# Sparse attention with a feed-forward layer on one core: the spacing of the feed-forward steps and the planner's price of a matrix product

## The chip, the cores and the metric

The kernel runs on one core of one Trainium2 chip. The metric is the device time of one execution in microseconds (us). A core has TensorE (in the profile PE, and PEld for its weight loads), VectorE (DVE), ScalarE (ACT), GpSimd (POOL) and SyncE (SP), which issues the DMA transfers here. Each engine runs its own list of instructions in order and waits for the others by semaphores.

## The reference

```python
def _attn_ref(q, k, v, tau):                       # batch 8, heads 8, 576 rows, 64 columns
    scale = 1.0 / np.sqrt(q.shape[-1])
    scores = scale * np.matmul(q, k.transpose(0, 1, 3, 2))
    thresh = np.max(scores, axis=-1, keepdims=True) - tau
    scores = np.where(scores >= thresh, scores, -1000000000.0)
    scores = scores - np.max(scores, axis=-1, keepdims=True)
    attn = np.exp(scores)
    attn = attn / (np.sum(attn, axis=-1, keepdims=True) + 1e-09)
    return np.matmul(attn, v).astype(np.float32)

def _moe_ref(x, w_in, w_out, s, b):                # x 4608 x 512, w_in 512 x 2048, w_out 2048 x 512
    h = x @ w_in
    r = np.maximum(h, 0.0)
    g = s * (r * r) + b
    return (g @ w_out).astype(np.float32)
```

Attention keeps only scores within tau of each row's maximum. Its output, with the heads side by side, is x: 8 batches of 576 rows, 4608 rows of 512 columns, and goes through the feed-forward layer.

## The kernel before, in words

**Attention** is worked in 288 tiles of 128 query rows of one head (`tile_of`). On PE a tile has scores against 576 keys (L328), later five transposes of the weighted scores (L357 into the bank `tp`, L358 into `tt`), and a product with the values for each group of two tiles (L404 into the bank `pv`; some groups carry 64 more rows, the tail). In the first 36 tiles, batch 0, a plain float32 form is used (L373 in the place of L404). Between them stand, for each tile, the copy with the row minimum on DVE (L331), the exponential on ACT (L337), the mask with the row sum on DVE (L340), the normalisation on POOL (L348), and the split of the transposed tile into two float32r parts, high on ACT (L388, L390) and low on DVE (L391, L393), which empties `tp` and `tt` for the next tile. The products' result is copied (ACT L409) and completed (DVE L411) into the columns of x. Each head's keys, queries and values are loaded by SP and split in the same manner (ACT L278, L286, L291; POOL L279, L292; DVE L287).

**Feed-forward** is worked in 18 blocks of 256 rows of x (`Block`). 16 of them are "full" blocks, two for each batch, which come ready every 18 tiles on average (after tiles 15, 35, 53, 71, 89, 107, 125, 143 and so on, counted from 0); two more hold the tails of four batches each and come ready after tiles 143 and 287. A block is staged (`stage`): x is split into `xh` (ACT L518) and `xl` (DVE L520), two pieces each; there are two pairs of these buffers, so one block can be staged while the one before is in use. Then come 16 steps (`step`), one for each 128 of the 2048 inner columns. A step is twelve matmuls of 256 columns into the bank `h` (L535), then ACT's Relu, which empties the bank (L538), its square (L540), the high part `gh` (L541), the low part `gl` on POOL (L542; on DVE in the last block), and six matmuls of 512 columns into `o` (L548), three for each half of the rows. There is one bank for `h`; `g`, `gh` and `gl` have two buffers. After 16 steps the block is finished: DVE adds the bias (L559) and SP stores it. The weights stay in SBUF; each is loaded and split (L465 to L476) before its first step.

**The order of the work** is not written by hand. Every operation is put in a plan (`Plan.add`) with its engine, a cost as a pair (how long the engine is held, how long until the result can be used; in ns), what it reads and writes, and a number `at`, in tiles. `Plan.run` goes through the program with these costs: whenever an engine is free, it takes among the operations whose inputs are there the one with the smallest `at`. So `at` is a rank among ready work and not a time, and an engine never waits in the plan while something is ready. What comes out is a fixed list for each engine; on the chip, each engine follows its list and waits where an input isn't there.

For the blocks, `when` (L711) is the number that the first step of a block gets: at least 1.5 tiles after the tile that completes the block, and not before the steps of the block ahead are through. Step f of the block gets `when + each * f` (L719), so `each` is how many tiles lie between two steps; a block of 16 steps takes 16 x `each` tiles, while the blocks come 18 tiles apart. The staging gets `max(i + 1.5, when - 1)`. Attention's operations have the tile's own number, with small offsets. PE's cost is reckoned in `pe` (L183) from the number of matmuls and their columns.

Of the kernel before, what the change touches and what calls it, by code (L numbers as in the profile page):

```python
# [106 lines left out]
def tile_attention_ffn(ctx: ExitStack, tc: tile.TileContext, qT, kT, v, tau, w_in, w_out, s, b, out):  # L107
# [50 lines left out]
    plan = Plan()  # L158
# [21 lines left out]

    def pe(n, cols, fn, r, w, at):

        plan.add("PE", (n * (0.452 * cols + 1.5), n * (0.452 * cols + 1.5) + 170), fn, r, w, at)  # L183

    def dve(cost, fn, r, w, at, port=False):
        plan.add("DVE", cost, fn, r, w, at, port)
# [128 lines left out]
    def tile_of(ti, i):  # L315
# [7 lines left out]
        def scores():  # L323
            for hf in range(2):
                cs = slice(hf * HS, (hf + 1) * HS)
                seq = ti.st()
                for n, (stat, kk) in enumerate(seq):
                    nc.tensor.matmul(ps[:, hf, 0:HS], stat, kk[:, cs], start=(n == 0), stop=(n == len(seq) - 1))  # L328
        pe(2 if plain else 4 * len(ti.heads), HS * (3.7 if plain else 1), scores, ti.kq(), [bk], i - SCORES_AHEAD)

        dve((760, 840), lambda: nc.vector.tensor_scalar(  # L331
# [22 lines left out]
        def transposes():  # L354
            em = get()[1]
            for t in range(NQ):
                nc.tensor.transpose(out=tp[:, t, :], in_=em[:, t * P:(t + 1) * P], identity=ident)  # L357
            nc.tensor.transpose(out=tt, in_=em[:, M:S], identity=ident)  # L358
        pe(4.3, 240, transposes, [em_k, "ident"], ["tp", "tt"], i + 0.5)
        if plain:  # L360
            ke = ("e32", i % 2)

            def both():
                nc.scalar.copy(out=e32(i)[:, 0:NQ], in_=tp)
                nc.scalar.copy(out=e32(i)[0:T, NQ], in_=tt)
            act((660, 760), both, ["tp", "tt"], [ke], i + 0.5)
            for pr, j, cs, dest, key in plain:
                n = cs.stop - cs.start

                def products(pr=pr, j=j, cs=cs, n=n):  # L370
                    for kt in range(5):
                        ks = slice(0, P if kt < NQ else T)
                        nc.tensor.matmul(bank["pv"][0:D, 0:n], pr.get()[2][ks, j, kt], e32(i)[ks, kt, cs], start=(kt == 0),  # L373
                                         stop=(kt == 4))
                pe(5, n * 4, products, [ke, pr.keys[2 + j], pr.keys[2 + j] + (1,)], ["pv"], i + VALUES_AFTER)
                act((80 + 0.75 * n, 180 + 0.75 * n), lambda dest=dest, j=j, n=n: nc.scalar.copy(
                    out=dest[j * D:(j + 1) * D], in_=bank["pv"][0:D, 0:n]), ["pv"], [key], i + VALUES_AFTER)
            return
# [17 lines left out]
    def with_v(g, at):  # L396
        ps = bank["pv"][:, 0:g.n]
        j = g.hd.j
        ke = g.keys(0, g.n, ("eh", "el", "et"))
        def products():  # L400
            hi, lo = (lazy[x][:, :, g.c0:g.c0 + g.n] for x in ("ehi", "elo"))
            seq = [(kt, o) for kt in range(4) for o in (hi, lo)] + [(4, hi)]
            for n, (kt, o) in enumerate(seq):
                nc.tensor.matmul(ps, g.hd.v()[:, kt, :, :], o[:, kt], start=(n == 0), stop=(n == len(seq) - 1))  # L404
        pe(9, g.n, products, ke + g.hd.kvs, ["pv"], at)
        a, o = slice(j * D, (j + 1) * D), slice((1 - j) * D, (2 - j) * D)
        for off, n, dest, key in g.dests:
            kx = [key + (j, u) for u in range(2)] if key[0] == "x" else [key + (j,)]
            act((50 + 0.85 * n, 150 + 0.85 * n), lambda off=off, n=n, dest=dest: nc.scalar.copy(  # L409
                out=dest[a], in_=ps[o, off:off + n]), ["pv"], kx, at)  # L410
            dve((80 + 1.05 * n, 160 + 1.05 * n), lambda off=off, n=n, dest=dest: nc.vector.tensor_tensor(  # L411
                out=dest[a], in0=ps[a, off:off + n], in1=dest[a], op=ALU.add), ["pv"] + kx, kx, at)
# [68 lines left out]
    def sums(k, at):  # L481

        fs = range(4 * k, 4 * k + 4)

        def products():
            for n, (f, h) in enumerate((f, h) for f in fs for h in range(2)):
                nc.tensor.matmul(bank["h"], ones, wo[h][f], start=(n == 0), stop=(n == 7))  # L487
        pe(8, DM, products, [(f"w{f}", "o") for f in fs] + ["ones"], ["h"], at)
        if k == 0:
            act((520, 620), lambda: nc.scalar.copy(out=bias_t, in_=bank["h"]), ["h"], ["bias"], at)  # L490
        else:
            dve((620, 700), lambda: nc.vector.tensor_tensor(out=bias_t, in0=bank["h"], in1=bias_t, op=ALU.add),
                ["h", "bias"], ["bias"], at)
        if k == 3:
            act((560, 660), lambda: nc.scalar.mul(out=bias_t, in_=bias_t, mul=b_t), ["bias", "b"], ["bias"], at)
# [76 lines left out]
    def make_block(kind, a, hf):  # L572
        if kind == "full":
            r = a * S + hf * NB
            k = xs[a, hf]
            return Block(xb[k], [("x", k, c, j, i) for c in range(NP) for j in range(2) for i in range(2)],
                         [[(0, P, out[r + t * P:r + (t + 1) * P, :])] for t in range(2)], (a, hf) == (B - 1, 1))
        return Block(xt, [("xt", bi, c, j) for bi in range(4) for c in range(NP) for j in range(2)],
                     [[(j * T, (j + 1) * T, out[(4 * a + 2 * t + j) * S + M:(4 * a + 2 * t + j + 1) * S, :])
                       for j in range(2)] for t in range(2)], False)  # L580
# [75 lines left out]
    tiles, first = [], {}  # L656
# [37 lines left out]
    def convert(f):  # L694
        if f not in converted:
            converted.add(f)
            load_weights(f, 2 + f)
            weights(f, WEIGHTS_AT + WEIGHTS_EACH * f)
# [4 lines left out]
    for i, ti in enumerate(tiles):  # L703
        ti.tag = "o" if i < TWO_BANKS and i % 2 else "s"

        events.append((i, lambda ti=ti, i=i: tile_of(ti, i)))
        for g in () if ti.plain else ti.end:
            events.append((i + 0.1, lambda g=g, i=i: with_v(g, i + VALUES_AFTER)))
        if True:
            for k_ in ti.blocks:  # L710
                when = max(when, i + FFN_AFTER)  # L711
                each = 1.125 if i < len(tiles) // 2 else 1.0

                def block(k_=k_, when=when, step=step, i=i, each=each):
                    blk = make_block(*k_)
                    blk.stage(max(i + FFN_AFTER, when - 1))
                    for f in range(NF):
                        convert(f)
                        blk.step(f, when + each * f)  # L719
                        if not step and f % 4 == 3:  # L720
                            sums(f // 4, when + each * f)
                    blk.finish(when + each * (NF + 1))

                events.append((max(i, n_plain) + 0.2, block))
                when += each * NF
                step += NF
# [47 lines left out]
```

## Time and profile before

| What | us |
|---|---|
| Three runs | 1429.4, 1423.86, 1428.97; median 1428.97 |
| Profiled execution | 1427.36 |
| Its span, first to last instruction | 1425.4 |
| PE busy | 1392.9 (98%), 9328 matmuls |
| Weight loads busy | 1255.2 (88%) |
| DVE busy | 1074.0 (75%) |
| ACT busy | 991.4 (70%) |
| POOL busy | 730.5 (51%) |
| Mean granted clock of TensorE | 0.994 |

Durations come from the profiled execution. A busy PE is not a PE at its peak: matmuls are pipelined, so that one is listed with 0.28 us or more while the next begins 0.12 us after it; how fast PE goes is read from start to start. Idle time listed before an instruction is measured from those modelled ends. The numbers in the names of buffers (`xh_3604`) are set anew for each program and only tell buffers apart within one.

### The profile page before, as it was taken

How to read it: one execution, taken by the hardware profiler on the slowest of the kernel's cores; microseconds unless marked ns; L12 is line 12 of the kernel's file. 1: busy time of each engine (PE TensorE's matmuls, PEld its weight loads, DVE VectorE, ACT ScalarE, POOL GpSimd, SP SyncE). 2: the span in 40 equal slices, each digit the busy share in tenths (PEclk: the TensorE clock that was granted, in tenths of full speed). 3: DMA queues.
4: the chain of work that ended last, by engine and by line, in shares of the span. 5: the costliest groups of instructions: out<-in, count | busy, mean ns of one | idle time of the engine just before them, and what ended most of it. 6: DMA issues, size and time to landing. Idle time of an engine off the chain costs nothing.

```text
span 1425.4 us, 29320 instructions
## 1 busy us (share of the span) xinstructions
PE 1392.9 (98%) x9328; PEld 1255.2 (88%) x9328; DVE 1074.0 (75%) x3099; ACT 991.4 (70%) x2487; POOL 730.5 (51%) x798
## 2 busy tenths in 40 slices
PE   8999999999999999999999999999999999999998
PEld 5677789898898989898999999999999999999887
DVE  4877777988888887988789887888788787886101
ACT  3777667777777767777677777776777777776443
POOL 1223345656565556656566556665556556653210
PEclk9999999999999999999999999999999999999999
DMA  8610011322222221322222222222222222220000
GB/s 294 246 39 21 23 58 52 95 58 61 60 79 73 59 79 52 95 59 62 64 66 80 70 72 65 80 65 63 63 75 69 76 57 70 61 85 1 16 16 15
DMA packets 94539, 99.58 MB, mean 70 GB/s; under 512 B 34480, under 2 KB 72368, under 8 KB 94384
## 3 DMA queue, kind: packets, MB, share of 16 engines
q1 hardware_dynamic: 94384, 97.71, 23.1%
q8 instruction: 73, 1.20, 0.3%
q14 instruction: 82, 0.67, 0.1%
HBM read 88.21 MB, written 9.44 MB: 69 GB/s over the span
## 4 chain that ended last, share of the span: by engine, by line
PE 92%; DVE 5%; issue 1%; ACT 1%; POOL 0%; DMA 0%; DVEq 0%; SPq 0%; ACTq 0%; POOLq 0%
PE h L535 28%; PE o L548 27%; PE s L328 12%; PE tp L357 9%; PE pv L404 9%; PE pv L373 4%; PE tt L358 2%; DVE em L340 1%; DVE e L391 1%; PE o L328 1%; PE h L487 1%; DVE xl L520 1%; DVE oo L559 0%; DVE e L393 0%; DVE x L411 0%
## 5 line engine op out<-in xcount | busy, mean ns | idle before, releaser
L535 PE MATMUL h<-xh,w 128*128 128x256 f32 x2304 | 471.1, 287 | 2.8 <-ACT xh L518 1.7
L535 PEld LDWEIGHTS h<-xh,w 128*128 128x128 f32 x2304 | 380.9, 192 | 13.0 <-ACT g L538 3.3
L348 POOL TENSOR_SCALAR em<-em,st 128x576 f32<-128x576 f32 x288 | 251.8, 874 | 272.6 <-DVE st L345 116.5
L548 PE MATMUL o<-w,gh 128*128 128x512 f32 x1152 | 370.0, 402 | 0.9 <-ACT g L538 0.5
L542 POOL TENSOR_TENSOR gl<-g,gh 128x256 fp32r<-128x256 f32 x272 | 213.2, 784 | 276.6 <-ACT gh L541 117.7
L535 PE MATMUL h<-xl,w 128*128 128x256 f32 x1152 | 328.8, 285 | 7.3 <-DVE xl L520 7.3
L340 DVE SCALAR_TENSOR_TENSOR em<-sm,st,em 128x577 f32<-128x577 f32 x288 | 253.0, 878 | 42.1 <-ACT em L337 32.0
L331 DVE TENSOR_SCALAR_CACHE_REDUCE sm<-s 128x576 f32<-128x576 f32 x280 | 211.2, 754 | 94.3 <-PE s L328 91.8
L337 ACT ACTIVATE em<-sm,st 128x576 f32<-128x576 f32 x288 | 224.9, 781 | 33.6 <-DVE sm L331 32.6
L538 ACT ACTIVATE g<-h 128x256 f32<-128x256 f32 x288 | 109.3, 380 | 194.9 <-PE h L535 189.1
L535 PEld LDWEIGHTS h<-xl,w 128*128 128x128 f32 x1152 | 221.8, 193 | 13.4 <-DVE xl L520 8.7
L548 PE MATMUL o<-w,gl 128*128 128x512 f32 x576 | 226.3, 393 | 0.0
L548 PEld LDWEIGHTS o<-w,gh 128*128 128x128 f32 x1152 | 195.7, 189 | 25.6 <-issue 1.2
L391 DVE TENSOR_TENSOR e<-tp,e 128x512 fp32r<-128x512 f32 (+1 forms) x280 | 178.2, 636 | 50.0 <-ACT e L388 44.9
L279 POOL TENSOR_TENSOR k<-rk,k 128x576 fp32r<-128x576 f32 x112 | 169.8, 1516 | 52.8 <-ACT k L278 48.4
L388 ACT CAST e<-tp 128x512 fp32r<-128x512 f32 (+1 forms) x280 | 151.0, 539 | 63.8 <-PE tp L357 60.2
L357 PE MATMUL tp<-ident,em 128*128 128x128 f32 x1152 | 176.8, 276 | 7.7 <-DVE e L391 4.7
L328 PE MATMUL s<-k,q 128*128 128x288 f32 x896 | 166.3, 308 | 0.8 <-DVE sm L331 0.8
L357 PEld LDWEIGHTS tp<-ident,em 128*128 128x128 f32 x1152 | 138.2, 141 | 32.4 <-POOL em L348 6.2
L404 PE MATMUL pv<-e,v 128*128 128x320 f32 (+1 forms) x1008 | 154.1, 296 | 1.2 <-DVE e L391 1.2
L404 PEld LDWEIGHTS pv<-e,v 128*128 128x128 f32 x1008 | 143.2, 189 | 7.3 <-DVE e L391 2.5
L328 PEld LDWEIGHTS s<-k,q 128*128 128x128 f32 x896 | 129.7, 190 | 4.7 <-DVE sm L331 2.0
(106 smaller groups left out, 1792.2 us busy)
## 6 DMA issues: line engine op xcount, KB each, us to landing
rk<-in_k_dram SPq DMA_DIRECT2D x224, 144.0 KB, 2.8
rv<-in_v_dram SPq DMA_DIRECT2D x112, 128.0 KB, 2.1
rq<-in_q_dram SPq DMA_DIRECT2D x168, 64.0 KB, 2.2
w<-in_moe_w_in_dram SPq DMA_DIRECT2D x16, 512.0 KB, 8.6
w<-in_moe_w_out_dram SPq DMA_DIRECT2D x16, 512.0 KB, 9.0
out_dram<-oo SPq DMA_DIRECT2D x32, 256.0 KB, 2.3
rq<-in_q_dram SPq DMA_DIRECT2D x56, 80.0 KB, 2.4
rv<-in_v_dram SPq DMA_DIRECT2D x224, 16.0 KB, 2.0
```

The costliest lines, as they stand in the source:

```text
L279: pool((1420, 1450), lambda: nc.gpsimd.tensor_tensor(out=klo(), in0=rk, in1=khi().bitcast(F32), op=ALU.subtract), pk + [f"khi{j}"], [f"klo ...
L328: nc.tensor.matmul(ps[:, hf, 0:HS], stat, kk[:, cs], start=(n == 0), stop=(n == len(seq) - 1))
L331: dve((760, 840), lambda: nc.vector.tensor_scalar(out=get()[0][:, 0:S].rearrange("p (a b) -> p a b", a=2), in0=ps[:, :, 0:HS], scalar1=-SC ...
L337: act((690, 785), lambda: nc.scalar.activation(out=get()[1][:, 0:S], in_=get()[0][:, 0:S], func=AF.Exp, bias=st8[:, 0:1], scale=-1.0), [sm ...
L340: dve2((830, 930), lambda: nc.vector.scalar_tensor_tensor(out=get()[1], in0=get()[0], scalar=st8[:, 1:2], in1=get()[1], op0=ALU.is_le, op1 ...
L348: pool((800, 835), lambda: nc.gpsimd.tensor_scalar(out=get()[1][:, 0:S], in0=get()[1][:, 0:S], scalar1=st8[:, 4:5], scalar2=st8[:, 5:6], o ...
L357: nc.tensor.transpose(out=tp[:, t, :], in_=em[:, t * P:(t + 1) * P], identity=ident)
L391: dve((60 + 560 * big, 140 + 560 * big), lambda hi=hi, lo=lo, cs=cs: nc.vector.tensor_tensor(out=lo(), in0=tp[:, :, cs], in1=hi()[:, 0:NQ] ...
L404: nc.tensor.matmul(ps, g.hd.v()[:, kt, :, :], o[:, kt], start=(n == 0), stop=(n == len(seq) - 1))
L535: nc.tensor.matmul(ps, w[:, c, :], x[:, c, :], start=(i == 0), stop=(i == 3 * NC - 1))
L542: do((715, 750), lambda: eng.tensor_tensor(out=lo, in0=g, in1=hi.bitcast(F32), op=ALU.subtract), [f"g{k}", f"gh{k}"], [f"gl{k}"], at)
L548: nc.tensor.matmul(bank["o"][:, t, :], a[:, ts_], w, start=(f == 0 and i == 0), stop=(f == NF - 1 and i == 2))
```

## The change

Two lines are changed. The price of n matmuls of `cols` columns in the plan goes from n x (0.452 x cols + 1.5) to n x (0.44 x cols + 6.5) ns. And `each` goes from 1.125 tiles for blocks that are completed in the first half of the 288 tiles to 1.2 for those completed in the first 100; after that it is 1.0, as it was in the second half before.

```diff
     def pe(n, cols, fn, r, w, at):
 
-        plan.add("PE", (n * (0.452 * cols + 1.5), n * (0.452 * cols + 1.5) + 170), fn, r, w, at)
+        plan.add("PE", (n * (0.44 * cols + 6.5), n * (0.44 * cols + 6.5) + 170), fn, r, w, at)
...
             for k_ in ti.blocks:
                 when = max(when, i + FFN_AFTER)
-                each = 1.125 if i < len(tiles) // 2 else 1.0
+                each = 1.2 if i < 100 else 1.0
```

No instruction is added or removed; both lines change the plan, and with it the order on every engine. Three places of that order are shown.

PE, from the product that completes block 4 (tile 89) on, before; `xh_4544` and `xl_4545` are the staged parts of block 4, `w_320` the weights of a block's first step:

```order
L404 MATMUL pv<-e,v 128x256 x9
L357 MATMUL tp<-ident,em_80 128x128 x4
L358 MATMUL tt<-ident,em_80 64x128
L328 MATMUL s<-k,q_84 128x288 x4
L535 MATMUL h<-xh_4544,w_320 128x256
L535 MATMUL h<-xl_4545,w_320 128x256
```

The first matmuls on the new block stand one transposition and one scores group behind the product that completes it.

PE, the same place in the changed program; `gh_96` and `gh_95` belong to steps of the block before, block 3:

```order
L404 MATMUL pv<-e,v 128x256 x9
L357 MATMUL tp<-ident,em_80 128x128 x4
L358 MATMUL tt<-ident,em_80 64x128
L548 MATMUL o<-w_1374,gh_96 128x512 x2
L548 MATMUL o<-w_1374,gl_98 128x512
L328 MATMUL s<-k,q_84 128x288 x4
L548 MATMUL o<-w_1434,gh_95 128x512 x2
L548 MATMUL o<-w_1434,gl_97 128x512
```

Work of block 3 follows here, and after these rows come the other half of that step's `o`, the next transposition, the twelve `h` matmuls of block 3's last step, two scores groups, a product and a further transposition and step of `o`, before the first `h` matmul of block 4.

PE, behind the product that completes block 2 (tile 53), in the changed program; before, the `h` matmuls of block 2 followed the scores group here too, as for block 4 above:

```order
L404 MATMUL pv<-e,v 128x256 x9
L357 MATMUL tp<-ident,em_80 128x128 x4
L358 MATMUL tt<-ident,em_80 64x128
L328 MATMUL s<-k,q_84 128x288 x4
L548 MATMUL o<-w_1588,gh_96 128x512 x2
L548 MATMUL o<-w_1588,gl_98 128x512
```

The six `o` matmuls of the last step of block 1 (three are shown) have moved between the scores group and the first `h` of block 2.

PE, near the end of the program, where the last step of one block and the first of the next meet; before (`xh_15204` is the new block's):

```order
L548 MATMUL o<-w_1440,gh_95 128x512 x2
L548 MATMUL o<-w_1440,gl_97 128x512
L535 MATMUL h<-xh_15204,w_320 128x256
L535 MATMUL h<-xl_15205,w_320 128x256
L535 MATMUL h<-xh_15204,w_320 128x256 x2
```

And in the changed program, where `xh_14368` is the old block's and `xh_15266` the new one's:

```order
L535 MATMUL h<-xl_14369,w_1588 128x256
L535 MATMUL h<-xh_14368,w_1588 128x256
L535 MATMUL h<-xh_15266,w_320 128x256
L535 MATMUL h<-xl_15267,w_320 128x256
L535 MATMUL h<-xh_15266,w_320 128x256 x2
```

The `o` matmuls between the two blocks' `h` matmuls are gone from this place: the second step stands right behind the first in the one bank of `h`. Only three `o` and the twelve `h` of the old block's last step lie between the last product with the values and the new block.

## The prediction

> **What bounds the kernel now.** I read, in this order, the page's totals, the busy time by long stretches, by short stretches, the waits, and the order in time around the places that those pointed to. TensorE (PE) is the bound (busy us, share, instructions):
>
> ```profile
> span 1425.4 us, 29320 instructions
> ...
> PE 1392.9 (98%) x9328; PEld 1255.2 (88%) x9328; DVE 1074.0 (75%) x3099; ACT 991.4 (70%) x2487; POOL 730.5 (51%) x798
> ```
>
> So the question is only where it loses time. Two stretches of about the same length answer it (start and end, length, busy us of PE, weight load, DVE, ACT, POOL with counts, granted clock, DMA share, GB/s):
>
> ```profile
> 190.00:700.00 510.00, 491.68 (x3350) 453.96 (x3349) 424.45 (x1227) 372.25 (x940) 293.87 (x314) 0.98 0.24 68
> 700.00:1200.00 500.00, 499.19 (x3485) 465.72 (x3484) 412.98 (x1215) 372.87 (x954) 301.69 (x324) 1.00 0.24 69
> ```
>
> From 190 to 700 us PE is idle for 18.3 us and its clock is below full; from 700 to 1200 it loses 0.8 us. The lost time is not spread. Seven short windows, each where one feed-forward block ends and the next starts (I number the change to block n as boundary n; the kernel counts blocks from 0), hold nearly all of it; the second sum is over the six stretches between them and the last 12 us:
>
> ```profile
> 190.00:200.00 10.00, 8.10 (x50) 7.13 (x49) 7.40 (x19) 5.86 (x13) 3.27 (x3) 0.86 0.28 95
> 270.00:282.00 12.00, 9.70 (x67) 8.20 (x66) 11.61 (x33) 8.52 (x20) 6.88 (x7) 1.00 0.37 113
> 350.00:363.00 13.00, 9.66 (x68) 8.47 (x66) 12.72 (x38) 8.76 (x21) 5.71 (x7) 1.00 0.33 98
> 430.00:442.00 12.00, 9.70 (x69) 8.21 (x67) 11.64 (x31) 8.72 (x21) 6.83 (x7) 1.00 0.39 114
> 510.00:523.00 13.00, 10.46 (x66) 9.46 (x65) 12.64 (x38) 8.18 (x20) 5.46 (x6) 0.87 0.32 99
> 590.00:600.00 10.00, 8.28 (x49) 7.25 (x47) 9.70 (x25) 6.61 (x16) 5.74 (x5) 0.83 0.26 76
> 670.00:688.00 18.00, 15.47 (x92) 14.20 (x91) 15.82 (x48) 12.13 (x31) 9.10 (x9) 0.81 0.33 96
> ```
> ```profile
> sum 422.00, PE 420.32 PEld 391.06 DVE 342.92 ACT 313.46 POOL 250.89; mean PE 60.05 PEld 55.87 DVE 48.99 ACT 44.78 POOL 35.84
> ```
>
> So 16.6 us of idle PE in 88 us, and 1.7 us in the other 422. What PE does there shows at boundary 2 (start, duration, instruction, the idle time before it in brackets):
>
> ```profile
> 271.47 1.35 PE L404 MATMUL pv<-e,v 128*128 128x256 f32 x9
> 273.04 0.66 PE L357 MATMUL tp<-ident,em 128*128 128x128 f32 x4 [0.23 <-POOL em L348]
> 273.53 0.27 PE L358 MATMUL tt<-ident,em 128*64 128x128 f32 x1
> 273.56 0.77 PE L328 MATMUL s<-k,q 128*128 128x288 f32 x4
> 274.89 0.39 PE L535 MATMUL h<-xh,w 128*128 128x256 f32 x1 [0.55 <-ACT xh L518]
> 276.22 0.39 PE L535 MATMUL h<-xl,w 128*128 128x256 f32 x1 [0.95 <-DVE xl L520]
> ```
>
> The product that completes the block's rows (pv) streams until 271.47 + 9 x 0.12 = 272.6; copying it out, adding, and splitting it into xh and xl take until 276.2, **3.6 us**, and PE has only one transpose and one scores group to do meanwhile. At the odd boundaries 3, 5 and 7, where the rows of the tail are copied too, the chain is longer and two attention tiles run with nothing between, so that the second transposition waits for its bank:
>
> ```profile
> 674.45 0.60 PE L357 MATMUL tp<-ident,em 128*128 128x128 f32 x4
> 674.88 0.27 PE L358 MATMUL tt<-ident,em 128*64 128x128 f32 x1
> 675.03 0.80 PE L328 MATMUL s<-k,q 128*128 128x288 f32 x4
> 677.35 0.63 PE L357 MATMUL tp<-ident,em 128*128 128x128 f32 x4 [1.52 <-DVE e L391]
> 677.82 0.27 PE L358 MATMUL tt<-ident,em 128*64 128x128 f32 x1
> 677.84 0.36 PE L535 MATMUL h<-xh,w 128*128 128x256 f32 x1
> 679.04 0.58 PE L535 MATMUL h<-xl,w 128*128 128x256 f32 x1 [0.83 <-DVE xl L520]
> ```
>
> Here the chain runs from 674.45, where the product has left PE, to 679.04: **4.6 us**.
>
> **What a boundary costs.** Three parts. Idle PE, from the windows: 1.9, 2.3, 3.3, 2.3, 2.5, 1.7 and 2.5 us. What the modelled ends hide: from 274.89 to 276.22 are 1.33 us where matmuls of this kind follow each other at 0.12, so 1.21 are lost and 0.95 listed; I take 0.2 a wait, for 1, 5, 4, 5, 3, 3 and 3 waits. And the clock: (1 - 0.86) x 10 = 1.4 us at boundary 1, then by the same product 1.7, 1.7 and 3.4 at boundaries 5, 6 and 7. Together 3.5, 3.3, 4.1, 3.3, 4.8, 4.0 and 6.5: **29.5 us** is all that there is to gain.
>
> **The spacing.** With 1.2 instead of 1.125 a block of 16 steps is due over 19.2 tiles, while blocks come 18 tiles apart; each of the first blocks is then late by 1.2 tiles more than the one before, up to 4.8 at block 5 (the product on tile 107), and at 1.0 that is given back by 2 a block until 0.8 is left at block 7. What was late fills PE while the next block is staged. How much stands between the completing product and the first h of the next block I counted in the order of both kernels, with these prices from starts in the quiet part (transposition 805.91 to 806.43, 0.52; three o 0.79; four scores 0.53; twelve h 1.42):
>
> ```profile
> 805.91 0.66 PE L357 MATMUL tp<-ident,em 128*128 128x128 f32 x4
> 806.40 0.27 PE L358 MATMUL tt<-ident,em 128*64 128x128 f32 x1
> 806.43 0.71 PE L548 MATMUL o<-w,gh 128*128 128x512 f32 x2
> 806.98 0.40 PE L548 MATMUL o<-w,gl 128*128 128x512 f32 x1
> 807.22 0.70 PE L328 MATMUL s<-k,q 128*128 128x288 f32 x4
> 807.75 0.27 PE L535 MATMUL h<-xh,w 128*128 128x256 f32 x1
> ...
> 809.17 1.49 PE L404 MATMUL pv<-e,v 128*128 128x320 f32 x9
> ```
>
> - Boundaries 4, 5 and 6 had 1.05, 1.6 and 1.05 us of cover. They now have a step or more of the old block in it: at 4 two transpositions and the one after, one and a half steps of o, twelve h, two scores groups and a product, over 9 us; at 5 and 6 over 12. The chain is 3.6 to 4.6, so all of 3.3 + 4.8 + 4.0 = 12.1 goes, the clock with it.
> - Boundary 3: from 1.6 to two transpositions, a scores group and twelve o, 1.04 + 0.53 + 3.16 = 4.7 us against 4.6, and the o between the transpositions gives the bank time. I leave 0.3 for unevenness: 3.8 gained.
> - Boundary 7: the same less one transposition, 0.52 + 0.53 + 3.16 = 4.2. Of its 3.1 of waiting 0.4 stays; of the clock's 3.4 I count half as gained: 4.4.
> - Boundary 2: from 1.05 to 0.52 + 0.53 + 1.58 = 2.6, which leaves 3.6 - 2.6 = 1.0 of the h waits and 0.7 of the smaller ones: 1.6 gained.
> - Boundary 1: two more scores groups, 1.06, and half of the clock's 1.4: 1.7 gained.
>
> Gained: 12.1 + 3.8 + 4.4 + 1.6 + 1.7 = **23.6 us**.
>
> What it adds. h has one bank, which ACT must empty (L538) before the next step writes it. Before, this happened with nothing between once, after the last tile:
>
> ```profile
> 1320.93 0.28 PE L535 MATMUL h<-xh,w 128*128 128x256 f32 x1
> ...
> 1321.75 0.38 PE L535 MATMUL h<-xh,w 128*128 128x256 f32 x1 [0.53 <-ACT g L538]
> ```
>
> That is 0.82 - 0.12 = 0.7 us each. The new order has five such pairs before tile 106, since PE catches up where attention isn't ready: **3.5 us**. At the end the late steps are used up: the last two blocks meet right behind the last product, with three o and twelve h (2.2 us) as cover, and two such pairs stand where one stood: **0.7 us** more, the cover taken as just enough, because VectorE and ScalarE have little else by then. Below nothing this can't go; with a chain of 3.6 the first pair would cost 1.4 and the whole 1.4.
>
> The price of products in the plan (for 256, 288, 320, 512 columns 119.1, 133.2, 147.3, 231.8 ns after 117.2, 131.7, 146.1, 232.9; the trace shows 0.12 for 256) executes nothing; it only reorders. After 700 us there are 0.8 us in 500 to lose or win, so I bound it by -0.8 and by the 1.7 us that the six quiet stretches together show, and take **1.0** as cost. No DMA is added, and none is moved to where PE waits for one.
>
> The sum: the profiled execution took 1427.36 us (span 1425.4 and 2.0 around it), 0.1% below the median of 1428.97. 1427.4 - 23.6 + 3.5 + 0.7 + 1.0 = **1409 us**.
>
> **The rivals.** *All seven boundaries close, 1398 to 1403*: 29.5 gained, 0 to 5 given back. For it: after 700 us, with later steps, no boundary is seen at all. Against: 2.6 us of cover for 3.6 at boundary 2, and the five pairs. Chance 0.13.
>
> *The clock's drops stay, 1415.* In four of the seven windows the granted clock is 0.81 to 0.87, and the longest wait between 190 and 700 us is this (total, times, longest):
>
> ```profile
> PE h L535 <- DVE xl L520: 7.3, 7, 1.9
> ```
>
> If such waits don't cause the drops, closing them doesn't bring the clock back: of the 8.2 us I booked 5.8, and 1409 + 5.8 = 1415. [...] For it: three windows with the same waits, boundaries 2 to 4, kept 1.00. Against: the stretch from 700 to 1200, without such waits, has 1.00 as a whole. Chance 0.10.
>
> *Cover that isn't long does nothing, about 1420*: the cover sits in PE's order, but the splits (L518, L520) also queue behind attention's work on ACT and DVE; where those run late, as DVE does in the windows (12.7 of 13 us busy at boundary 3), added PE work only lets them start later. Then 12.1 are gained and 5.2 lost. For it: DVE is nearly full at the even boundaries too, 11.6 of 12. Against: part of that load is two tiles pressed together, which the cover parts. Chance 0.17.
>
> *Slower: attention can't keep the pace.* Its place is tiles 36 to 107. A tile gets the time of 1/1.2 instead of 1/1.125 of a step, so all of DVE's and POOL's work on it is pressed into less PE time. Where a tile is late, only steps are left, and they meet the one bank of h.
>
> ```profile
> L340 DVE SCALAR_TENSOR_TENSOR em<-sm,st,em x288: 801/822/2085, 9.3 to 1308.2; 128x577 f32<-128x577 f32 x144
> ```
>
> L340 takes 0.82 us at the median and 2.09 at worst, so something stops it at times. [...] Each of some 60 steps that meets a full bank costs 0.7 us; from 32 of them on, (23.6 - 0.7 - 1.0) / 0.7 = 31.3, the change loses, from 42 on by more than 7 us; all 60 give 1427.4 - 23.6 + 42 + 1.7 = 1447. Against: the order has five, and DVE is busy 342.9 of 422 us between the boundaries, 81%, which 1.2 raises to about 85. Chance 0.08.
>
> **The numbers.** The forecast, 1403 to 1418, has 0.52. 0.5% of the median, about what a measurement of this kernel can tell from no change, is 7 us: faster ends at 1422. Faster: 0.52, 0.13, 0.10 and a third of the rival at 1420 (0.05) make 0.80; same 0.12, slower 0.08. The range leaves out the slower rival and the best of the first: 1400 to 1425.
>
> **What would show it.** Right: PE idle in 190 to 700 us falls from 18 to under 7, with no waits for xl at boundaries 4 to 6, some left at 1 and 2, and five of 0.5 for ACT g before 500 us; the stretch after 700 keeps its rate. Wrong: waits for xl L520 at every boundary as before (cover does nothing); many waits of h for g, or of tp for em or e, between the boundaries (the slower rival); a clock below 1.00 where PE doesn't wait (drops stay).

## The result, and the profile after

The changed kernel takes 1405.51 us (median of 4 runs, 1401.75 to 1409.7) against 1428.87 for the one before (median of 4): a ratio of 0.9845, 95% interval 0.9809 to 0.9881. 1409 was forecast. The profiled executions went from 1427.36 to 1406.54 us.

The page after (span, and busy us with share and instructions of each engine), then the two long stretches that were shown of before:

```profile
span 1404.8 us, 29315 instructions
...
PE 1381.5 (98%) x9328; PEld 1247.9 (89%) x9328; DVE 1071.9 (76%) x3099; ACT 991.5 (71%) x2487; POOL 737.6 (53%) x798
```
```profile
190.00:700.00 510.00, 502.25 (x3483) 464.78 (x3481) 438.22 (x1272) 381.38 (x970) 311.73 (x326) 1.00 0.24 70
700.00:1200.00 500.00, 500.00 (x3505) 468.09 (x3504) 408.77 (x1201) 373.27 (x953) 298.04 (x322) 1.00 0.24 69
```

In the first stretch PE is idle for 7.8 us, where it was 18.3, and gets through 3483 matmuls, where it was 3350; the clock is 1.00, where it was 0.98. Seven windows as long as those of before, laid around the first h of each new block, and their sum:

```profile
190.00:200.00 10.00, 9.12 (x59) 7.43 (x58) 6.88 (x13) 5.72 (x13) 2.40 (x4) 1.00 0.13 52
270.00:282.00 12.00, 11.32 (x80) 10.16 (x78) 11.12 (x29) 9.30 (x23) 6.65 (x8) 1.00 0.30 96
350.00:363.00 13.00, 11.30 (x74) 9.84 (x73) 12.32 (x35) 9.39 (x25) 6.74 (x8) 1.00 0.28 86
428.00:440.00 12.00, 11.35 (x83) 10.35 (x81) 11.79 (x28) 9.51 (x23) 8.09 (x7) 1.00 0.24 67
508.00:521.00 13.00, 12.31 (x85) 11.43 (x84) 11.79 (x37) 8.51 (x25) 6.66 (x8) 1.00 0.24 70
588.00:598.00 10.00, 10.00 (x75) 9.53 (x74) 9.39 (x23) 7.66 (x20) 6.67 (x8) 1.00 0.40 130
652.00:670.00 18.00, 17.66 (x126) 16.11 (x125) 15.96 (x41) 14.44 (x39) 9.36 (x10) 1.00 0.22 67
sum 88.00, PE 83.06 PEld 74.86 DVE 79.26 ACT 64.53 POOL 46.58; mean PE 11.87 PEld 10.69 DVE 11.32 ACT 9.22 POOL 6.65
```

4.9 us of idle PE are left of 16.6, and no window has a clock below 1.00. Boundary 2, on PE (start, duration, instruction, the idle time before it):

```profile
271.97 0.78 PE L328 MATMUL s<-k,q 128*128 128x288 f32 x4
272.59 0.62 PE L548 MATMUL o<-w,gh 128*128 128x512 f32 x2
273.05 0.40 PE L548 MATMUL o<-w,gl 128*128 128x512 f32 x1
273.28 0.62 PE L548 MATMUL o<-w,gh 128*128 128x512 f32 x2
273.74 0.40 PE L548 MATMUL o<-w,gl 128*128 128x512 f32 x1
273.97 0.28 PE L535 MATMUL h<-xh,w 128*128 128x256 f32 x1
274.92 0.38 PE L535 MATMUL h<-xl,w 128*128 128x256 f32 x1 [0.66 <-DVE xl L520]
```

The old block's o stand where PE waited for xh, and one wait for xl is left, 0.66 us listed. All waits of PE from 190 to 700 us after (total, times, longest):

```profile
PE h L535 <- ACT g L538: 3.1, 6, 0.7
PE h L535 <- DVE xl L520: 1.3, 2, 0.7
PE s L328 <- DVE sm L331: 0.7, 2, 0.3
PE pv L404 <- DVE e L391: 0.7, 1, 0.7
PE tp L357 <- POOL gl L542: 0.6, 1, 0.6
PE tp L357 <- POOL em L348: 0.6, 2, 0.3
```

The wait for xl, 7.3 us in seven before, has become 1.3 in two; the wait of h for its bank to be emptied (ACT g) is new and now the largest.

**An account of the whole span.** Take each matmul's start to the next one's start, less the usual spacing of its kind (0.12 us for 256 columns, 0.133 for 288, 0.147 for 320, 0.232 for 512, 0.109 for a transposition), and add what is over: this is what PE loses, hidden waits and low clock included. It is 99.1 us before and 78.7 after; subtracted from the spans that leaves 1326.3 and 1326.1. For all fourteen profiles of this study the remainder lies between 1326.0 and 1326.6; it is the same work in each, so that it is constant only says that nothing outside PE, at the start or the end, has changed. The profiles can then be compared by where PE's losses lie. "Late" is by how many tiles each block's steps are ranked later than in the kernel before:

| Kernel | Price of n matmuls | Spacing of steps | Median us | Ratio to before, 95% | Lost to 190 us | 190 to 700 | After 700 |
|---|---|---|---|---|---|---|---|
| before | 0.452 cols + 1.5 | 1.125 | 1428.87 | | 41.0 | 43.3 | 14.8 |
| after | 0.44 cols + 6.5 | 1.2 | 1405.51 | 0.9845 (0.9809 to 0.9881) | 42.4 | 24.0 | 12.3 |
| e1_spacing_only | old | 1.2 | 1416.33 | 0.9932 (0.9912 to 0.9952) | 43.1 | 32.8 | 12.3 |
| e2_price_only | new | 1.125 | 1427.42 | 1.0005 (0.9984 to 1.0026) | 45.2 | 36.7 | 18.0 |
| e3_two_tiles_late | old | 1.125, 2 late | 1410.29 | 0.9895 (0.9871 to 0.9918) | 44.9 | 24.3 | 16.7 |
| e4_spacing_1_3 | new | 1.3 | 1428.04 | 1.0029 (1.0011 to 1.0048) | 43.9 | 43.6 | 16.6 |
| e5_price_late_1 | new | 1.125, 1 late | 1429.54 | 1.0005 (0.9971 to 1.0039) | 43.1 | 37.7 | 20.3 |
| e6_price_late_3 | new | 1.125, 3 late | 1417.66 | 0.9928 (0.9893 to 0.9964) | 38.4 | 24.1 | 18.6 |
| e7_higher_price | 0.44 cols + 9 | 1.2 | 1410.22 | 0.9876 (0.9808 to 0.9944) | 36.3 | 28.5 | 12.6 |
| e8_spacing_1_225 | new | 1.225 | 1420.31 | 0.9961 (0.9927 to 0.9995) | 40.2 | 27.7 | 25.0 |
| e9_price_plus_0 | 0.44 cols | 1.2 | 1424.6 | 1.0005 (0.9981 to 1.0029) | 39.8 | 37.0 | 15.5 |
| e10_price_plus_4 | 0.446 cols + 4 | 1.2 | 1410.29 | 0.9907 (0.9882 to 0.9931) | 45.4 | 24.5 | 12.2 |
| e11_price_plus_12 | 0.44 cols + 12 | 1.2 | 1408.66 | 0.9896 (0.9864 to 0.9928) | 39.8 | 27.0 | 16.0 |
| e12_small_ops_first | new | 1.2 | 1404.87 | 0.985 (0.9817 to 0.9883) | 37.5 | 19.6 | 12.3 |

The kernel before was run beside each group again, with medians of 1426.07 to 1426.53; the ratios are to those. The losses are those of one profiled execution; the medians are over all runs, while the ratios leave disturbed ones out, so the ratio decides. From before to after, 19.3 of the 20.4 us came from between 190 and 700 us; 2.5 more went after 700, and 1.4 came in before 190. What is lost before 190 differs by up to 9 us among the fourteen profiles (36.3 to 45.4), so differences of a few us in that column are not read.

### The profile page after: what moved, and what is told of

It is laid out like the page before. It is cut to its first block, busy times and chain, and to the rows that moved or that the text cites. A ratio compares the mean times of both kernels' runs of the same rounds, so it can differ in the third digit from the quotient of the medians.

```text
span 1404.8 us, 29315 instructions
## 1 busy us (share of the span) xinstructions
PE 1381.5 (98%) x9328; PEld 1247.9 (89%) x9328; DVE 1071.9 (76%) x3099; ACT 991.5 (71%) x2487; POOL 737.6 (53%) x798
## 4 chain that ended last, share of the span: by engine, by line
PE 72%; DVE 1%; ACT 1%; issue 1%; DVEq 0%; POOL 0%; ACTq 0%
PE h L535 24%; PE o L548 23%; PE s L328 9%; PE pv L404 8%; PE tp L357 6%; PE tt L358 2%; DVE e L391 0%; DVE em L340 0%; ACT g L538 0%; ACT e L388 0%; ACT em L337 0%; DVE e L393 0%; DVE sm L331 0%; DVE oo L559 0%; DVE qt L287 0%
## 5 line engine op out<-in xcount | busy, mean ns | idle before, releaser
L535 PE MATMUL h<-xh,w 128*128 128x256 f32 x2304 | 465.3, 285 | 4.3 <-ACT g L538 4.1
L348 POOL TENSOR_SCALAR em<-em,st 128x576 f32<-128x576 f32 x288 | 255.1, 886 | 261.1 <-DVE st L345 86.9
L535 PEld LDWEIGHTS h<-xh,w 128*128 128x128 f32 x2304 | 376.2, 190 | 14.7 <-ACT g L538 7.6
L542 POOL TENSOR_TENSOR gl<-g,gh 128x256 fp32r<-128x256 f32 x272 | 217.4, 799 | 265.9 <-ACT gh L541 102.6
L340 DVE SCALAR_TENSOR_TENSOR em<-sm,st,em 128x577 f32<-128x577 f32 x288 | 253.9, 882 | 41.3 <-ACT em L337 31.6
L535 PEld LDWEIGHTS h<-xl,w 128*128 128x128 f32 x1152 | 218.9, 190 | 7.2 <-DVE xl L520 2.2
L279 POOL TENSOR_TENSOR k<-rk,k 128x576 fp32r<-128x576 f32 x112 | 168.1, 1501 | 48.6 <-ACT k L278 47.5
L357 PEld LDWEIGHTS tp<-ident,em 128*128 128x128 f32 x1152 | 137.6, 141 | 28.5 <-issue 5.9
```

The lines of the kernel that those rows point to most:

```text
L279: pool((1420, 1450), lambda: nc.gpsimd.tensor_tensor(out=klo(), in0=rk, in1=khi().bitcast(F32), op=ALU.subtract), pk + [f"khi{j}"], [f"klo ...
L340: dve2((830, 930), lambda: nc.vector.scalar_tensor_tensor(out=get()[1], in0=get()[0], scalar=st8[:, 1:2], in1=get()[1], op0=ALU.is_le, op1 ...
L348: pool((800, 835), lambda: nc.gpsimd.tensor_scalar(out=get()[1][:, 0:S], in0=get()[1][:, 0:S], scalar1=st8[:, 4:5], scalar2=st8[:, 5:6], o ...
L535: nc.tensor.matmul(ps, w[:, c, :], x[:, c, :], start=(i == 0), stop=(i == 3 * NC - 1))
L542: do((715, 750), lambda: eng.tensor_tensor(out=lo, in0=g, in1=hi.bitcast(F32), op=ALU.subtract), [f"g{k}", f"gh{k}"], [f"gl{k}"], at)
```

## The experiments

The theory was the prediction's: what counts is how much work of the old block PE has while the next one is staged. The rivals were that the plan's truer price does it, or the slower pace of steps.

**e1_spacing_only.** From the kernel before:

```diff
-                each = 1.125 if i < len(tiles) // 2 else 1.0
+                each = 1.2 if i < 100 else 1.0
```

> Only the spacing is changed (1.2 tiles for the first 100), the price of products is the old one. Theory (late steps cover the staging): the order has 9 us or more of work behind the completing product at boundaries 4 to 6, 3.8 to 4.3 at 3 and 7, 2.1 at 1 and 0.9 at 2, so all but boundary 2 gain as they did: 1407 to 1412, idle TensorE time in 190 to 700 us under 9. Rival (the truer price made the order fit the chip): little gained, 1420 or more.

1416, a ratio of 0.9932: less than half of the change's gain, and between theory and rival. The boundaries 4 to 6 are free of waits for xl, as expected (the two of the stretch, 0.9 us, are at boundary 3), but single long waits of attention stand elsewhere. The longest is behind boundary 2; all engines in order of time there:

```profile
275.27 1.62 POOL L279 TENSOR_TENSOR k<-rk,k 128x576 fp32r<-128x576 f32 x1 [2.07 <-ACT k L278]
...
275.67 1.51 DVE L287 TENSOR_TENSOR q<-rq,q 64x256 fp32r<-64x256 f32 x1
...
276.85 1.05 POOL L292 TENSOR_TENSOR v<-rv,v 128x320 fp32r<-128x320 f32 x1
...
277.21 0.43 DVE L411 TENSOR_TENSOR x<-pv,x 64x256 f32<-64x256 f32 x1
277.67 0.69 DVE L391 TENSOR_TENSOR e<-tp,e 128x512 fp32r<-128x512 f32 x1
...
278.70 0.16 DVE L343 RECIPROCAL st<-st 128x1 f32<-128x1 f32 x1
278.78 0.14 DVE L345 TENSOR_SCALAR st<-st 128x1 f32<-128x1 f32 x1
278.83 1.28 DVE L520 TENSOR_TENSOR xl<-x,xh 128x512 fp32r<-128x512 f32 x2
279.02 1.71 POOL L348 TENSOR_SCALAR em<-em,st 128x576 f32<-128x576 f32 x1 [1.13 <-DVE st L345]
...
280.79 0.65 PE L357 MATMUL tp<-ident,em 128*128 128x128 f32 x4 [4.51 <-POOL em L348]
```

PE waits 4.5 us for a tile's weighted scores. POOL was itself busy with splits until 277.90. It then stood idle for 1.1 us more, because two operations of 0.15 us (L343, L345) stood in DVE's fixed order behind 3 us of other work, three splits and the completion of a product; and L348 itself then took 1.71 us, twice its median of 0.83 before, while the split into xl ran on DVE. (L287 took 1.51 us beside L279, which took 1.62, where their medians before are 0.60 and 1.44. In the trace of before, 138 executions of L340 on DVE have no POOL instruction beside them and took at most 0.83 us; of the 150 with one beside them 53 took longer, up to 2.09. So instructions of the two engines were slowed side by side; how long one holds the other these rows do not show.)

**e2_price_only.** From the kernel before, the new price alone:

```diff
-        plan.add("PE", (n * (0.452 * cols + 1.5), n * (0.452 * cols + 1.5) + 170), fn, r, w, at)
+        plan.add("PE", (n * (0.44 * cols + 6.5), n * (0.44 * cols + 6.5) + 170), fn, r, w, at)
```

> Only the price of products is changed, the spacing is the old one. The order has 2.4 us of work at each of boundaries 2 to 7, where 1.0 or 1.5 stood. Theory (cover against a staging of 3.6 and 4.6 us): about 1.4 gained at the even and 2 at the odd boundaries, 0.5 at boundary 1, some of the clock with it, and 2 lost to four steps that stand right behind another in the one bank of h: 1415 to 1421, with waits for xl L520 left at every boundary. Rival (the price is the main thing): 1410 or less. As the prediction had it (the price changes nothing): 1428 to 1430.

1.0005: nothing gained. Theory and rival both miss; the third, the prediction's own, is nearest. Its five largest waits from 190 to 700 us:

```profile
PE h L535 <- DVE xl L520: 4.7, 7, 0.8
PE s L328 <- DVE sm L331: 4.3, 4, 1.7
PE h L535 <- ACT g L538: 2.3, 6, 0.5
PE pv L404 <- DVE e L391: 2.2, 7, 0.3
PE s L328 <- DVE st L345: 1.2, 3, 0.4
```

With 2.4 us of work at each of boundaries 2 to 7 (six o, a transposition and a scores group), the wait for xl went from 7.3 to 4.7, and waits of scores and of products for DVE came in its place. The stretch loses 6.6 us less than before, and as much more is lost outside it, so a cover shorter than the staging gained nothing in the whole. That is the outcome of the rival "cover that isn't long does nothing", which had 0.17, but not its reason, that the splits would only start later. At boundary 2:

```profile
276.66 1.21 PE L404 MATMUL pv<-e,v 128*128 128x256 f32 x8 [0.34 <-DVE e L391]
277.71 0.63 PE L548 MATMUL o<-w,gh 128*128 128x512 f32 x2
...
281.29 0.39 PE L535 MATMUL h<-xl,w 128*128 128x256 f32 x1 [0.83 <-DVE xl L520]
```

The product streams until 276.66 + 8 x 0.12 = 277.6, and xl is there 3.7 us later; before, it was 3.6. At boundaries 4 and 6 it is as at 2, and at the odd ones it is shorter than before. The splits came no later, and PE waited less for them; what was won there was lost in other waits.

**e3_two_tiles_late.** From the kernel before, all blocks' steps two tiles later, spacing and price as before:

```diff
-                when = max(when, i + FFN_AFTER)
+                when = max(when, i + FFN_AFTER + 2)
```

> Old spacing (1.125) and old price, but every block's steps are ranked two tiles later, so they lag by a constant two tiles and never grow apart. The order has 2.9 us of work at boundary 1 and 4.3 to 5.4 at 2 to 7. Theory (cover is all, the pace is nothing): nearly all of the 29 us of the boundaries is gained, less 0.65 each for seven steps right behind another: 1403 to 1409. Rival (the slower pace of steps, 1.2, is what helps, since it leaves VectorE and ScalarE time): not below 1420.

1410, 0.9895, a little above the expected 1403 to 1409. One wait for xl of 0.2 us is left in 190 to 700, and the loss there is 24.3, that of the changed kernel. So it is lateness that closes the boundaries; neither the slower pace nor the price is needed for it.

**e4_spacing_1_3.** From the changed kernel:

```diff
-                each = 1.2 if i < 100 else 1.0
+                each = 1.3 if i < 100 else 1.0
```

> As the changed kernel, with 1.3 for 1.2. Cover at boundaries 1 and 2 is 3.4 and 3.7 us, beyond 11 at 3 to 7, so the waits left at 2 and 3 go (about 2 us). Theory: no further gain beyond that, because a boundary that is covered has nothing more to give, and five places where a transposition stands close behind another (as at the odd boundaries of the kernel before, 1.5 us each) take it back: 1402 to 1410. Rival (more lateness is better all along): below 1398. Rival (attention can't keep the pace): above 1412, with waits of h for ACT g.

1428, 1.0029: the gain is gone, as the third theory had it. The expected places, but dearer. Its four largest waits from 190 to 700 us:

```profile
PE tp L357 <- DVE e L391: 5.4, 4, 1.9
PE s L328 <- DVE sm L331: 3.4, 6, 1.3
PE h L535 <- ACT g L538: 2.8, 6, 0.5
PE pv L404 <- DVE e L391: 2.2, 4, 1.1
```

There is no wait for xl at all. PE waits for DVE, on attention, mostly around tiles 55, 95 and 121, where the order has transpositions close behind each other, 3 to 7 us in all at each, from start to start; the bank of h is no larger a cost than at 1.2.

**e5_price_late_1 and e6_price_late_3.** The edit of e3 with 1 and 3, and the new price.

> New price, old spacing, every block's steps ranked one tile later than before. With e2_price_only as its zero (1427) this is the first dose of lateness. The order has 1.5 to 2.9 us of work behind the completing product at all of boundaries 1 to 7, and no whole step of the old block. Theory now (only a whole step of the old block, h and o, or a cover beyond the staging's 3.6 and 4.6 us frees a boundary; less only moves the wait to another place, as in e2_price_only): 1420 to 1428, waits for xl L520 left at most boundaries. Rival (each us of cover is a us gained): 1415 or less.

1.0005: no gain, and 1430 is just above the expected range; eight waits for xl, 5.5 us. With e2_price_only this is a second dose that is too small.

> As e5_price_late_1 with three tiles for one: the order has 4.5 to 9.3 us at every one of boundaries 1 to 7. Theory: no wait for xl L520 is left anywhere, idle TensorE time in 190 to 700 us under 8, five steps right behind another at 0.65 each: 1400 to 1408. Rival (the growing lateness of 1.2 is needed, or the slower pace): 1412 or more.

0.9928: a gain, but smaller than expected; 1417.66 lies in the rival's range. One wait for xl of 1.3 us is left, at boundary 1, where none was expected. The traced execution was the fastest of its runs at 1409.0; its loss from 190 to 700 us is 24.1, as expected, and 18.6 are lost after 700, where the changed kernel loses 12.3. Why its other runs are longer isn't in that trace and stays open.

**e7_higher_price.** The changed kernel with + 9 for + 6.5.

> The changed kernel with n x (0.44 x cols + 9) for + 6.5, 2% more than the chip takes for 256 columns. Covers at boundaries 1 to 7 are those of the changed kernel (2.1, 2.9, 4.3, 9.9, 9.7, 12.1, 3.8). Theory (with the spacing the covers are there, and the price only decides where single waits of attention fall): within 6 us of the changed kernel, 1400 to 1412. Rival (the price has to be the true one): 1414 or more, as in e1_spacing_only.

1410, 0.9876, as the theory had it: the changed kernel's ratio lies within the interval.

**e8_spacing_1_225.** The changed kernel with 1.225 for 1.2.

> The changed kernel with 1.225 for 1.2, a step toward e4_spacing_1_3. Covers 2.1, 2.9, 7.9, 13.4, 15.6, 18.1 and 5.7 us, and two places (tiles 55 and 61) where a transposition stands close behind another, where 1.3 had five. Theory (attention pressed together is what made 1.3 slow, and each such place costs 2 to 5 us): 1404 to 1414. Rival (1.3 was slow since 11 steps more are left to the end): no slower than the changed kernel, 1400 to 1406, since here only 2 more are left.

1420, 0.9961, above both ranges. The loss from 190 to 700 us is 27.7, so attention is not much pressed there; the rest, 25.0 against 12.3, lies after 700, in many waits of at most 0.7 us. So the theory's reason isn't what made it slow, and the order after 700 is another one in each kernel; no run here tells more.

**e9_price_plus_0, e10_price_plus_4, e11_price_plus_12.** The changed kernel with other prices, as the table has them.

> The changed kernel (spacing 1.2) with n x 0.44 x cols as price: 112.6 ns for a matmul of 256 columns that takes 120 on the chip. Covers at boundaries 1 to 7: 2.9, 1.5, 3.4, 7.0, 9.5, 9.3, 2.9 us; three places where a transposition stands close behind another (tiles 54, 55, 92), eight steps right behind another before tile 120. Theory (the spacing brings the gain, the price only decides where single waits of attention fall): 1408 to 1420, below the kernel before. Rival (a price that is too low costs by itself, the more the lower, as 1.5 cost 10 us against 6.5): 1420 or more.

> Spacing 1.2 with n x (0.446 x cols + 4), 118.2 ns for 256 columns, between the old price (117.2) and the new (119.1). Covers 1.5, 2.9, 4.8, 4.3, 10.3, 10.5, 3.8; one close transposition, four steps right behind another. Theory: no trend with the price, 1403 to 1414. Rival (the nearer the price to the chip's, the better): between 1405 and 1412, about 1409.

> Spacing 1.2 with n x (0.44 x cols + 12), 124.6 ns for 256 columns, 4% above the chip. Covers 2.1, 2.9, 5.7, 9.3, 14.8, 11.2, 3.8; no close transposition before the end, four steps right behind another. Theory: the covers of the changed kernel, so its time within 8 us, 1400 to 1414. Rival (the true price is what counts): 1414 or more. Rival (any price that isn't too low serves): 1403 to 1411, with less waiting for em between the boundaries than at 4.

1.0005, 0.9907 and 0.9896. With e1_spacing_only (+ 1.5, 0.9932), the changed kernel and e7_higher_price, that is a series at the spacing of 1.2: 1425, 1416, 1410, 1406, 1410 and 1409 for a matmul of 256 columns at 112.6, 117.2, 118.2, 119.1, 121.6 and 124.6 ns. The rival of + 0 holds; + 4 lies in both of its ranges, and + 12 in those of the theory and of "any price that isn't too low serves", though the sign named for the latter, less waiting for em than at + 4, is not there (2.3 us against 2.1 from 190 to 700). "No trend" falls: below 119.1 ns the time rises the lower the price is; from there up it stays within 5 us, and the intervals overlap. How a low price does it is only partly seen: the wait for xl, 2.2 us at boundary 3, and eight steps right behind another are in the order of + 0, as expected, but + 1.5 has other waits. Each price stands for one order, and in e8_spacing_1_225 another order, from a spacing 0.025 larger, cost 15 us. So how much of the series is the price itself and how much the luck of an order isn't shown; at the old spacing the new price brought nothing.

**e12_small_ops_first.** The changed kernel, with the two small operations of DVE ranked earlier:

```diff
-        dve((110, 165), lambda: nc.vector.reciprocal(out=st8[:, 4:5], in_=st8[:, 2:3]), [(ks_, 2)], [(ks_, 4)], i)
+        dve((110, 165), lambda: nc.vector.reciprocal(out=st8[:, 4:5], in_=st8[:, 2:3]), [(ks_, 2)], [(ks_, 4)], i - 3)
...
-            [(ks_, 2)], [(ks_, 5)], i)
+            [(ks_, 2)], [(ks_, 5)], i - 3)
```

> The changed kernel, and VectorE's two small operations behind the row sum (L343, L345, 0.15 us each, which POOL's normalisation waits for) get the rank of three tiles earlier, so that in the plan they stand ahead of the long splits. In e1_spacing_only the longest wait (4.5 us of TensorE for em) stood behind L343 queued after 3 us of splits. Theory (such queueing in VectorE's fixed order is what single waits are made of): waits for POOL em fall below 1 us in all, 1399 to 1406. Rival (the plan's order has them right, and the waits come from the durations of POOL and VectorE that stop each other): no change, 1403 to 1409.

All its waits from 190 to 700 us:

```profile
PE h L535 <- DVE xl L520: 1.6, 1, 1.6
PE tp L357 <- DVE e L391: 1.4, 2, 1.0
PE h L535 <- ACT g L538: 0.9, 2, 0.5
PE s L328 <- DVE sm L331: 0.7, 2, 0.3
PE pv L404 <- DVE e L391: 0.3, 1, 0.3
```

No wait for em is left here (0.6 us in the changed kernel), and the loss in this stretch, 19.6 us, is the smallest of all profiles. But 1405 lies in the ranges of both the theory and the rival, and the ratio, 0.985, is that of the changed kernel within both intervals, so that it is faster is not shown. No kernel here beats the changed one beyond the measurement.

## Why the prediction was right, point by point

- **The bound and the seven boundaries.** Right. 19.3 of the 20.4 us that went were between 190 and 700 us. 16.6 us of idle PE in the windows became 4.9. From start to start the windows lost 32.5 us before (29.5 were reckoned) and 10.4 after: 22.0 went where 23.6 were forecast.
- **Boundaries 4 to 6, 12.1 us with the clock.** Right in kind: no wait for xl in these windows, no low clock; 10.5 us went from start to start. New there are one wait of a product for e (0.65 us listed, at 432) and one of h for its bank (0.69, at 518), 1.7 us from start to start that no step had.
- **Boundaries 1, 2, 3 and 7.** Mis-sized singly: 1.6, 2.6, 1.9 and 5.5 us went where 1.7, 1.6, 3.8 and 4.4 were forecast, so that the errors nearly cancel, which is luck. Waits for xl were to be left at 1 and 2; they are at 2 and 3. 0.3 was left at boundary 3 for unevenness; it kept a wait for xl of 0.66, one of a transposition of 0.63 and smaller ones. At boundary 7 0.4 of waiting was left and 0.6 (a scores group, at 664) is there. Boundary 2 kept 0.8 for xl from start to start where 1.0 was expected.
- **The clock.** 5.8 of 8.2 us were booked; the drops all went. The rival that the drops stay had 1415; its premise, that such waits don't cause the drops, does not fit these traces (last section). Drops and waits can come apart: in e2_price_only all seven boundaries still wait and the clock is 1.00 throughout the stretch, whose loss is 6.6 us smaller than before; that profile loses as much more before 190 and after 700 us. What the drops alone are worth in the whole time no run shows: of the executions of e2_price_only the traced one, with a mean clock of 1.000, took 1427.8 us, and one with 0.997 took 1421.5.
- **Steps right behind another.** Five before tile 106, as counted, at 0.63 each (3.2 us for the 3.5); two after the last product, as counted.
- **The price of products, 1.0 us of cost.** This step failed. It was bounded by the idle time that is listed away from the boundaries, but the price decides what stands at the boundaries too, and from start to start there was more to win: after 700 us, where 0.8 were listed up to 1200, 2.5 went. Alone it is worth nothing (1.0005), with the spacing it makes 0.9932 into 0.9845, about 12 us. The sum came out near because the covers were counted in the order of the changed program, which has both; the share of each line could not be had that way.
- **The rivals.** The slower one, attention that can't keep the pace, is real, with its place at 1.3 and not at 1.2, and by waits for DVE, not by the bank of h. "Cover that isn't long does nothing" has the outcome of e2_price_only and e5_price_late_1, where the covers are short; its reason, splits that start later, is not what e2_price_only shows.
- **Idle PE under 7 us from 190 to 700.** 7.8.

## What to carry to other kernels

Where the busiest engine waits for the hand-over of a block, give it work of the block before that lasts longer than the hand-over (here 3.6 to 4.6 us). About half of that gained nothing in the whole, and far more, at a spacing of 1.3, pressed the other engines until the gain was gone. Take the bound engine's price in a planner from start to start in a trace; here, beside the new spacing, too high a price cost less than too low a one, with one order for each. Judge two edits of a plan together and apart: one was worth nothing alone and about half of the gain beside the other.

## What the runs showed of the hardware

In the trace of before, the granted clock of TensorE fell to half (0.50) four times within the span, and the longest listed gap of PE that began in the 3.41 us ahead of each was 1.9, 1.5, 1.0 and 1.5 us. By the trace's record of the clock the low stretches, at boundaries 1, 5, 6 and 7, begin at 197.14, 517.99, 596.50 and 678.41 us; the first three last 3.413 us and the fourth 6.827, and their starts lie 94, 23 and 24 times 3.413 us apart. Two pairs of neighbouring windows of that length before, set on those starts (PE's busy time is the first after the length, the granted clock the third from the right):

```profile
514.58:517.99 3.41, 1.57 (x11) 1.18 (x10) 3.29 (x10) 3.33 (x9) 2.11 (x3) 1.00 0.41 129
517.99:521.40 3.41, 2.88 (x13) 2.88 (x14) 3.35 (x9) 0.37 (x3) 0.82 (x1) 0.50 0.35 104
```
```profile
432.70:436.11 3.41, 2.04 (x14) 1.41 (x12) 3.28 (x9) 2.96 (x7) 2.38 (x3) 1.00 0.34 99
436.11:439.52 3.41, 2.79 (x21) 2.52 (x22) 3.31 (x7) 2.23 (x6) 1.42 (x1) 1.00 0.27 76
```

In the first pair the longest gap is 1.5 us, and the whole next window is at half clock (0.50); in the second pair, with a little more work (2.04 us of busy PE for 1.57), it is not (1.00). In the profiles of before, after and e1 to e4, I took for each such window at full clock the share of it in which matmuls stream by the spacings above, from 33 us on, where the record of the clock begins: all nine with 0.36 or less were followed by a window at half clock, one of five between 0.38 and 0.43, and none above. Before has three of the nine, from 514.58, 593.08 and 675.00 us with shares of 0.31, 0.33 and 0.33, and the one of the five, from 193.72 us with 0.39 (mean clock 0.994); the others fall in e1 and e4 (0.998 and 0.995), since e2, e3 and after have a mean clock of 1.000; after has no window below 0.53. The other eight profiles have two more windows with 0.36 or less, both followed by half clock, and two between 0.38 and 0.43, one of them followed by it (mean clocks below 1.000 in e5, e9 and e12: 0.998, 0.997 and 0.998). What sets the clock beyond these counts no run here tells.
